# A gated mix of two attentions: left tokens laid over the key weights, output weights requested last

## The chip, the cores and the metric

The kernel runs on one NeuronCore of a Trainium2 chip (trn2). Its engines are TensorE (PE in the profile, with PEld for its weight loads), VectorE (DVE), ScalarE (ACT), GpSimd (POOL) and SyncE (SP), each with its own instruction stream; SP and ACT also request the DMA transfers here, which 16 DMA engines carry out. The metric is the device time of one execution in microseconds (us). Before the change it is 951.8 us, the median of six runs from 949.97 to 952.97.

## The reference, cut to what matters

Two attentions, A and B, are computed from the same input of 2048 tokens of 512 numbers and mixed by a gate that each token computes from itself.

```python
def _A_ref(x, mem0, Wq, Wk, Wv, Wo, seg_len):      # 32 heads of 128, 8 memory tokens, segments of 32
    mem = mem0
    for s in range(n_seg):                          # 64 segments, one after the other
        h = jnp.concatenate([mem, xs], axis=1)      # 8 memory tokens and 32 tokens
        q, k, v = h @ Wq, h @ Wk, h @ Wv            # per head
        p = softmax(where(mask, q @ k.T * scale, -1e9))
        o = (p @ v) @ Wo
        mem = o[:, :M, :]                           # the next segment's memory
        outs.append(o[:, M:, :])
def _B_ref(x, wq, wk, wv, wo, beta):               # 32 heads of 16, 4 stretches of 512 tokens
    for s in range(4):
        a_dot = softmax(qs @ ks.T * scale + mask) @ vs
        a_mem = (phi(qs) @ M) / (phi(qs) @ z + 1e-6)
        outs.append(g * a_mem + (1 - g) * a_dot)
        M = M + phi(ks).T @ vs; z = z + phi(ks).sum()
    return o @ wo
g = sigmoid((x * gate_w).sum(-1))
return g * _A_ref(...) + (1 - g) * _B_ref(...)
```

In A every segment needs the memory of the segment before, so the 64 segments form one chain. B can be computed at any time.

## The kernel before, in words

**Emission.** The kernel is planned in Python. `Prog` keeps one list of operations for each engine; an operation states which resources it reads and writes, and `emit` (line 162) turns that into semaphore waits. An engine carries its list out strictly in the order in which the plan wrote it.

**The projections (0 to about 75 us).** `plan_loads` (line 451) asks SP for the input and B's weights (wkB, wvB, wqB), and returns a list of 29 delayed requests: eight pieces of 512 KB each of Wk, Wq and Wv and four of 1 MB of Wo, requested by ACT, and at last woB, eight small requests by SP. `b_projections` (line 570) returns 64 pieces, of four stretches: keys, values and queries of B, each a product of four matmuls on PE, a cast on ACT or DVE to a staging buffer (stgk, stgq, stgp in rings of three or four; V17 for the values) and a store to a scratch in HBM by SP (kTd, qTd, pQd, vd). The last four pieces are the values of the last stretch; the last element only finishes what is outstanding. The loop at line 365 runs the pieces, and behind a piece it takes requests from the list (line 379): two behind every three pieces while more than five are left, then one behind every fifth piece. Whatever is left is requested behind the loop (line 381). Wo_sb lies over the input x_sb, so a Wo request may not come before the input has been transposed.

**Shared memory.** The buffers of the projections (`in_p`, line 282) and those of the segments (`in_a`, line 291) use the same stretch of SBUF. `v.under` (line 298) finds for each segment buffer the projection buffers under it, with a margin of 64 bytes, and the first user of a segment buffer waits for the last users of those (`over`, line 334). In bytes from the start of the stretch, a partition's share of the projection buffers is wkB 0 to 4096, wqB to 8192, wvB to 12288, V17 to 16640, phK to 20736, and small ones and the staging buffers behind. Of the segment buffers, LN_sb starts at 0, KTL at 2048, QTL at 6144, VL at 10240, xL at 14336, KN_sb at 14592, QN_sb at 16640.

**Left tokens.** The last eight tokens of each segment are called left tokens here. For four segments at a time (a group), `left_units` (line 925) copies their input to xL on POOL (line 928) and computes their K, Q and V in six products of 16 matmuls (line 911, KL0 to VL1). A product of K or Q is cast to LN_sb (line 945), by ACT or DVE as the table A_ENG says, and turned ("flipped") by a transpose on DVE (lines 923 and 949) to KTL or QTL; V is cast to VL. Group 0 is computed between the projections and segment 0; group g + 1 is spread over group g.

**A segment.** `segment` (line 1091) defines units and runs them in the order that a list names; A_ORDER (line 856) has four lists, for the four segments of a group (called the first to the fourth kind). Q, K and V are half products (Q0x, Q0y and so on), q0, k0, v0 are their casts to QN_sb, KN_sb and V_sb, TQ and TK the flips, S the scores, X the exponential, M the sums, L their reciprocals, N and n the normalising, PV and PL the products with the values, E their casts to OT_sb (line 1217), W the products with Wo (line 964), H and l the split of the result in a high and a low part, F the sum over four head groups (line 986), hm the cast of the new memory, ax that of the output rows, oL a copy of the left tokens' columns on POOL.

Other names are fillers, which put B's work and the tails between: bS (scores, line 746), bE (exponential, line 760, with a mask on POOL, line 767), bP (product with the values, line 793), bT (the rest), Fc and Ff (begin a left product or the like), Fe (its cast). A filler looks whether there is something for it to do at that point (lines 1252 to 1274) and otherwise does nothing. How many bS are due by the end of a segment is fixed (line 1250). B's keys and values come back from HBM by `load` (line 704): for the first job SP is asked for them right behind the projections (line 384).

**Banks.** PE writes to eight PSUM banks, handed out by `Banks` in the order of the plan; a product waits for the cast that emptied its bank.

Of the kernel before, what the change touches and what calls it, by code (L numbers as in the profile page):

```python
# [7 lines left out]
BF16 = mybir.dt.bfloat16  # L8
# [215 lines left out]
def build(nc, es, A_x, A_mem0, A_Wq, A_Wk, A_Wv, A_Wo, B_wq, B_wk, B_wv, B_wo, B_beta, gate_w, out, dbg=None):  # L224
# [28 lines left out]
    def sbt(name, shape, dt, stack):  # L253
        return stack.enter_context(nc.sbuf_tensor(name, shape, dt))

    def alloc(stack, *specs):
        at, spans = 0, {}
        for name, shape, dt, n in specs:
            t = [sbt(name + (str(i) if n else ""), shape, dt, stack) for i in range(max(n, 1))]
            setattr(v, name, t if n else t[0])  # L260
            size = 4 if dt == F32 else 2
            for k in shape[1:]:
                size *= k
            for i in range(max(n, 1)):
                spans[name + (str(i) if n else "")] = (at, at + size)
                at += size
        return spans
# [20 lines left out]
    v.stg = {"k": v.stgk, "q": v.stgq, "p": v.stgp}  # L288
    v.x_sb = v.Wo_sb[:, 0:NTT, :]
    esA = ExitStack()  # L290
    in_a = alloc(esA, ("LN_sb", [128, 2, 512], BF16, 0), ("KTL", [128, H // 2, SEG, 2], BF16, 2), ("QTL", [128, H // 2, SEG, 2], BF16, 2),
          ("VL", [128, 2, 512], BF16, 2), ("xL", [128, C, SEG], BF16, 0), ("KN_sb", [128, 2, 512], BF16, 0), ("QN_sb", [128, 2, 512], BF16, 0),
          ("KT_sb", [128, H // 2, SEG, 2], BF16, 0), ("QT_sb", [128, H // 2, L, 2], BF16, 0), ("V_sb", [128, 2, 512], BF16, 0),
          ("P_sb", [128, 2, 224], BF16, 0), ("R_sb", [128, 2, 160], F32, 0),
          ("OT_sb", [128, H, L], BF16, 0), ("OTL", [128, H, SEG], BF16, 2),
# [17 lines left out]
    def Rs(name):  # L313
        if name not in R:
            R[name] = Res(name)
            home = v.home(name)
            if home:
                R[name].readers = over(home)
        return R[name]
# [42 lines left out]
    weights = plan_loads(v, A_x, A_mem0, A_Wq, A_Wk, A_Wv, B_wq, B_wk, B_wv, B_wo, B_beta, gate_w)  # L362
    pieces = b_projections(v)
    bat = v.bat = BAttn(v)
    for n in range(len(pieces)):
        if n % 4 == 0 and n < 16:
            x_chunk(v, n // 4)
        if n == 9:
            sigmoid(v, v.beta_sb[:, :], v.gB_sb, v.omgB_sb, "gB", [Rs("beta")])
            for src, dst, res in ((v.gB_sb, v.gBp, "gB"), (v.omgB_sb, v.omgBp, "omgB")):  # L370
                for j in range(4):
                    q = slice(32 * j, 32 * j + 32)
                    P.op("gp", lambda g, src=src, dst=dst, q=q, j=j: g.tensor_copy(dst[q, :], src[q, :].rearrange("p (f j) -> p f j", j=4)[:, :, j]),
                         reads=[Rs(res)], writes=[Rs(res + "p")], name="%sp%d" % (res, j))
            v.late_const()
        if n == 24:
            plan_gates(v)
        pieces[n]()
        if weights and (n % 3 if len(weights) > 5 else n % 5 == 0):
            weights.pop(0)()  # L380
    while weights:
        weights.pop(0)()
# [118 lines left out]
def x_chunk(v, k):  # L501

    P, Rs, BK, C = v.P, v.Rs, v.BK, v.C
    for h in range(2):
        bk = BK.take()
        tiles = (4 * k + 2 * h, 4 * k + 2 * h + 1)

        def f(pe, bk=bk, tiles=tiles):
            ins = None
            for n, i in enumerate(tiles):  # L510
                for c in range(C):
                    o = (n * C + c) * 128
# [15 lines left out]
def sigmoid(v, src, g, o, res, reads):  # L528

    P, rg = v.P, v.Rs(res)  # L530
    P.op("act", lambda a: a.activation(g[:, :], src, ACT.Exp, scale=-1.0), reads=reads, writes=[rg], name=res + "_e")
    P.op("dve", lambda d: d.tensor_scalar(g[:, :], g[:, :], 1.0, None, op0=ALU.add), reads=[rg], writes=[rg], name=res + "_a")
    P.op("dve", lambda d: d.reciprocal(g[:, :], g[:, :]), reads=[rg], writes=[rg], name=res + "_r")
    P.op("dve", lambda d: d.tensor_scalar(o[:, :], g[:, :], -1.0, 1.0, op0=ALU.mult, op1=ALU.add), reads=[rg], writes=[v.Rs("om" + res)],
         name="om" + res)


def plan_gates(v):

    P, Rs, BK, C, NTT = v.P, v.Rs, v.BK, v.C, v.NTT  # L540
    bk = BK.take()
    P.op("pe", lambda pe, bk=bk: pe.transpose(v.pb16[bk][:, 0:C], v.gwr_sb[0:C, :], v.ident[0:C, 0:C]),
         reads=[Rs("gwr"), Rs("ident")], writes=[v.rbank[bk]], name="gwtr")
    v.evac("dve", v.gw_sb[:, :], v.pb16[bk][:, 0:C], [bk], [Rs("gw")], "gwev")
    BK.give(bk)
    bk = BK.take()

    def f_gate(pe, bk=bk):
        ins = None
        for i in range(NTT):  # L550
            for c in range(C):
                ins = pe.matmul(v.pb[bk][:, i:i + 1], v.xT[:, c, i * 128:(i + 1) * 128], v.gw_sb[:, c:c + 1],
                                start=(c == 0), stop=(c == C - 1))
        return ins
    P.op("pe", f_gate, reads=[r for k in range(4) for r in x_res(v, k)] + [Rs("gw")], writes=[v.rbank[bk]], name="gate_mm")
    sigmoid(v, v.pb[bk][:, 0:NTT], v.g_sb, v.omg_sb, "g", [v.rbank[bk]])
    BK.give(bk)
    bk = BK.take()

    def f_m0tr(pe, bk=bk):  # L560
        ins = None
        for c in range(C):
            ins = pe.transpose(v.pb16[bk][:, c * v.M:(c + 1) * v.M], v.mem0_sb[0:v.M, c * 128:(c + 1) * 128], v.ident[0:v.M, 0:v.M])
        return ins
    P.op("pe", f_m0tr, reads=[Rs("mem0"), Rs("ident")], writes=[v.rbank[bk]], name="mem0tr")
    v.evac("dve", v.hT[0][:, :, 0:v.M], v.pb16[bk][:, 0:C * v.M].rearrange("p (c t) -> p c t", t=v.M), [bk], [Rs("hTm0_0"), Rs("hTm0_1")], "memT0")
    BK.give(bk)
# [120 lines left out]
class BAttn:  # L688
# [157 lines left out]
    def finish(self, sb, f):  # L846
# [8 lines left out]

A_ORDER = [o.split() for o in (
    """
    Q0x K0x bE bE bT Q0y Fe K0y Q1x q0 bE k0 bE Q1y TQ0 bP K1x Fe bE TK0 K1y Fe S0 q1 TQ1 X0 bS V0x bS k1 M0 TK1 bE V0y S1 bE bE V1x X1 v0
    V1y M1 L0 n0 Fe Fc N0 L1 v1 PV0 PL0 N1 E0b n1 E0a Fe Fc PV1 PL1 W0a W0b E1a E1b Fe Fe W1a bE W1b bP bS H0 Fe Fe Ff Fc l0 H1 bP bE l1
    bE Fe Ff F0 hm0 ax0 bS F1 hm1 Fe oL Fe ax1 bS Ff bE Fe bE Ff""",  # L860
    """
    K0x Q0x bE bE bE Q0y K0y bE Q1x q0 Fe bE Q1y TQ0 bE Fe Fe bP k0 K1x bE q1 bE TK0 TQ1 K1y k1 bE TK1 bE S0 X0 bS Fe V0x M0 bE V0y S1 V1x
    bE L0 V1y N0 n0 Fe v0 X1 Fe M1 L1 v1 Fc PV0 n1 N1 PL0 bE Fc E0b bE E0a PV1 Fe PL1 W0a E1b bT W0b E1a W1a oL W1b Fe Fe bP H0 bS bS Fe
    Ff Fc l0 bP bP bE H1 l1 Fe bE Ff F0 bE bS hm0 F1 hm1 bS ax1 bE ax0 bE Fe""",
    """
    Q0x bT Fe Q0y q0 bE K0x bP bE TQ0 K0y k0 Q1x Q1y TK0 K1x K1y S0 q1 Fe V0x bS TQ1 Fe X0 k1 Fe TK1 M0 V0y Fe S1 bE V1x V1y L0 X1 v0 bE
    M1 L1 N0 v1 Fe Fe Fc bE PV0 N1 n0 PL0 E0b bE E0a n1 Fe bT Fc PV1 PL1 W0a W0b E1b E1a W1a W1b bE Fe Fc H0 bP l0 bS H1 Fe Ff oL bP l1 bE
    Fe F0 bS hm0 ax0 F1 Ff hm1 ax1 Fe Fe""",
    """
    Q0x Fe bS bT bE Q0y bE Fe bE q0 K0x TQ0 bP K0y bE k0 Fe Fe Fc Q1x Q1y Fc Fc q1 K1x Fc TK0 TQ1 K1y k1 TK1 S0 X0 bE bS Fe V0x M0 V0y S1  # L870
    bE V1x L0 X1 N0 Fe v0 n0 V1y Fe M1 v1 PV0 L1 N1 bE n1 bE PL0 Fe E0b PV1 Fe E0a PL1 bP W0a E1b bT W0b E1a Fe bE W1a W1b bE H0 bS bE l0
    Fe H1 Ff bP l1 Ff bT bE F0 hm0 bE ax0 bS F1 Fe bS hm1 Fe Ff ax1 Fc Fe Fe oL Ff""")]
A_ENG = dict(E0a="dve", E0b="act", E1a="act", E1b="dve", H0="act", H1="dve", K0="act", K1="dve", KL0="act", KL1="act", L0="dve",
             L1="act", OL="dve", Q0="act", Q1="act", QL0="dve", QL1="act", V0="act", V1="dve", VL0="act", VL1="dve", ax="act", hm="act",
             n="gp")


def plan_a(v, nseg):
# [13 lines left out]
    ngrp = (nseg + 3) // 4  # L892
    ORDER, ENG = DEV.get("order") or A_ORDER, DEV.get("eng") or A_ENG
    if len(ORDER) != 4:
# [503 lines left out]
```

## Time and profile before

| | us |
|---|---|
| median of six runs | 951.8 (949.97 to 952.97) |
| the profiled execution | 949.97 |
| its span in the profile | 948.2 |
| PE busy | 882.9 (93%) |
| DVE busy | 658.5 (69%) |
| ACT busy | 581.3 (61%) |
| POOL busy | 249.2 (26%) |

The profile is of one execution on the chip. Times are in us from the start of the span, in the timeline the start and the length of a merged group of equal instructions; what stands in brackets behind is how long the engine had been idle before and what ended that. L911 is line 911 of the kernel. A line with SPq or ACTq is a request of a DMA transfer, not the transfer. The granted clock is the share of full speed that PE was given. Matmul ends are modelled, so busy PE time is not PE at its peak.

### The profile page before, as it was taken

The page shows a single profiled execution, that of the slowest core. Times are in us where ns is not written, and L with a number is a line of the kernel's source. Part 1 is how long each engine was busy: PE and PEld are TensorE (multiplying, and loading weights), DVE is VectorE, ACT ScalarE, POOL GpSimd, SP SyncE. Part 2 cuts the span into 40 slices and gives each one's busy share as a digit, 9 for nine tenths or more (in the row PEclk, how much of TensorE's full clock was granted, in tenths as well). Part 3 has the DMA queues.
Part 4 walks back from the last instruction along what each step waited for, and adds up shares of the span by engine and source line. Part 5 has one row for each costly group of instructions (what it writes and reads, how often), then busy time and mean ns, then how long its engine had stood idle before and what let it go on. Part 6 is the DMA issues. An engine that isn't in the chain of part 4 may idle for free.

```text
span 948.2 us, 51802 instructions
## 1 busy us (share of the span) xinstructions
PE 882.9 (93%) x23167; PEld 467.0 (49%) x23173; DVE 658.5 (69%) x1374; ACT 581.3 (61%) x1291; POOL 249.2 (26%) x554
## 2 busy tenths in 40 slices
PE   7994989999998999999999999999999999999985
PEld 4442545545555555545555555545554555544443
DVE  3573657667676687777677687777777787777664
ACT  3352667666676666666666666666666666665443
POOL 2620223222222223232232223232322132222110
PEclk9997999999999999999999999999999999999999
DMA  9996000000001121100102011100101010000110
GB/s 297 377 383 206 5 17 17 18 18 12 24 16 38 26 50 36 29 15 18 25 15 55 26 44 24 30 22 11 42 16 49 21 44 22 26 4 9 37 37 8
DMA packets 67718, 51.38 MB, mean 54 GB/s; under 512 B 34592, under 2 KB 64424, under 8 KB 67496
## 3 DMA queue, kind: packets, MB, share of 16 engines
q1 hardware_dynamic: 59880, 31.29, 12.0%
q10 hardware_dynamic: 7616, 16.78, 4.8%
q8 instruction: 182, 2.98, 1.3%
q14 instruction: 40, 0.33, 0.1%
HBM read 33.47 MB, written 14.57 MB: 51 GB/s over the span
## 4 chain that ended last, share of the span: by engine, by line
PE 82%; DVE 8%; ACT 5%; issue 3%; DMA 2%; POOL 0%; ACTq 0%; DVEq 0%; POOLq 0%
PE ps L911 43%; PE ps L964 13%; PE ps L746 5%; PE ps L1197 3%; PE ps L630 2%; PE ps L986 2%; PE ps L605 2%; DVE WL L975 2%; ACT PT L760 2%; PE ps L1136 2%; PE ps L793 2%; PE ps L1162 2%; DMA scr_pQd<-stgp 1%; PE ps L1210 1%; PE ps L1129 1%
## 5 line engine op out<-in xcount | busy, mean ns | idle before, releaser
L760 ACT ACTIVATE PT<-ps 128x1024 bf16<-128x1024 f32 x160 | 164.0, 1025 | 7.4 <-PE ps L746 6.1
L767 POOL TENSOR_SCALAR_AFFINE_SELECT PT<-PT 128x512 bf16<-128x512 bf16 (+1 forms) x96 | 75.7, 788 | 274.9 <-ACT PT L760 261.0
L911 PE MATMUL ps<-Wv_sb,hT 128*32 128x512 bf16 x2048 | 142.9, 381 | 0.0
L911 PE MATMUL ps<-Wk_sb,hT 128*32 128x512 bf16 x2048 | 141.5, 379 | 0.0
L911 PE MATMUL ps<-Wq_sb,hT 128*32 128x512 bf16 x2048 | 138.0, 380 | 0.0
L964 PE MATMUL ps<-Wo_sb,OT_sb 128*32 128x512 bf16 x2048 | 123.2, 380 | 0.2 <-DVE OT_sb L356 0.2
L923 DVE STREAM_TRANSPOSE QT_sb<-QN_sb 128x256 f32<-128x256 f32 x128 | 56.6, 442 | 83.8 <-ACT QN_sb L354 83.8
L1187 POOL TENSOR_TENSOR P_sb<-P_sb,R_sb 128x64 bf16<-128x64 bf16 x128 | 52.8, 412 | 187.7 <-DVE R_sb L1170 77.2
L354 ACT ACTIVATE QN_sb<-ps 128x512 bf16<-128x512 f32 x128 | 76.8, 600 | 40.6 <-PE ps L911 39.7
L354 ACT ACTIVATE OT_sb<-ps 128x320 bf16<-128x320 f32 x128 | 56.0, 437 | 66.9 <-PE ps L1210 66.3
L1145 ACT ACTIVATE P_sb<-ps 128x224 bf16<-128x224 f32 x128 | 45.7, 357 | 66.5 <-PE ps L1136 65.1
L975 DVE TENSOR_TENSOR WL<-ps,WH 128x256 bf16<-128x256 f32 x128 | 54.3, 424 | 43.1 <-ACT WH L354 39.3
L356 DVE CAST OT_sb<-ps 128x320 bf16<-128x320 f32 x128 | 61.6, 482 | 26.2 <-PE ps L1210 25.7
L1170 DVE RECIPROCAL R_sb<-ps 128x160 f32<-128x160 f32 x64 | 74.1, 1157 | 7.8 <-PE ps L1162 2.6
L911 PEld LDWEIGHTS ps<-Wk_sb,hT 128*32 128x32 bf16 x2048 | 52.2, 97 | 46.0 <-ACT KN_sb L354 1.6
L911 PEld LDWEIGHTS ps<-Wq_sb,hT 128*32 128x32 bf16 x2048 | 50.5, 96 | 46.7 <-ACT hT L354 4.2
L964 PEld LDWEIGHTS ps<-Wo_sb,OT_sb 128*32 128x32 bf16 x2048 | 49.4, 96 | 44.5 <-ACT OT_sb L354 5.1
L746 PE MATMUL ps<-QTj,KTj 32*128 32x256 bf16 (+1 forms) x768 | 62.6, 254 | 3.4 <-ACT PT L760 2.7
L923 DVE STREAM_TRANSPOSE KT_sb<-KN_sb 128x256 f32<-128x256 f32 x128 | 56.6, 442 | 11.5 <-ACT KN_sb L354 7.9
L354 ACT ACTIVATE WH<-ps 128x256 bf16<-128x256 f32 x64 | 24.6, 384 | 56.6 <-PE ps L964 48.3
L354 ACT ACTIVATE LN_sb<-ps 128x512 bf16<-128x512 f32 (+1 forms) x80 | 40.6, 507 | 25.2 <-PE ps L911 14.1
L1181 DVE TENSOR_TENSOR P_sb<-P_sb,R_sb 128x160 bf16<-128x160 bf16 x128 | 45.9, 358 | 12.7 <-ACT R_sb L1177 0.9
(132 smaller groups left out, 1620.2 us busy)
## 6 DMA issues: line engine op xcount, KB each, us to landing
Wk_sb<-in_A_Wk_dram ACTq DMA_DIRECT2D x8, 512.0 KB, 6.0
Wq_sb<-in_A_Wq_dram ACTq DMA_DIRECT2D x8, 512.0 KB, 6.9
Wv_sb<-in_A_Wv_dram ACTq DMA_DIRECT2D x8, 512.0 KB, 6.8
Wo_sb<-in_A_Wo_dram ACTq DMA_DIRECT2D x4, 1024.0 KB, 11.6
scr_vd<-V SPq DMA_DIRECT2D x16, 136.0 KB, 6.2
Vj<-scr_vd SPq DMA_DIRECT2D x32, 68.0 KB, 2.4
Wo_sb<-in_A_x_dram SPq DMA_DIRECT2D x4, 512.0 KB, 7.4
scr_kTd<-stgk SPq DMA_DIRECT2D x16, 128.0 KB, 7.8
```

The lines of the kernel that those rows point to most:

```text
L354: P.op("act", lambda a: a.activation(dst, src, ACT.Copy), reads=[v.rbank[k] for k in bks], writes=dres, name=name)
L356: P.op("dve", lambda d: d.tensor_copy(dst, src), reads=[v.rbank[k] for k in bks], writes=dres, name=name)
L746: ins = pe.matmul(v.pb[bks[x]][:, 256 * e + o:256 * e + o + w], KT[e][r, 128 * kc:128 * (kc + 1)], QT[r, q0:q0 + w], start=True, stop=True ...
L760: P.op("act", lambda a: a.activation(pt[:, :, :], v.ps[:, bks[0]:bks[1] + 1, :], ACT.Exp, scale=v.SCALE_B), reads=[v.rbank[b] for b in bks ...
L767: P.op("gp", lambda g: g.affine_select(mv, mv, [[0, mv.shape[1]], [1, 128]], ALU.is_ge, 0.0, base=0, channel_multiplier=-1), reads=[rp], w ...
L911: ins = pe.matmul(pb[bk][SEG * j:SEG * (j + 1), :], lhs(c), cols(w, j) if split else w[:, 512 * j:512 * (j + 1)], start=(c == 0), stop=(c ...
L923: P.op("dve", lambda d: d.transpose(to, src), reads=reads, writes=writes, name=name)
L964: ins = pe.matmul(pb[bk][SEG * j:SEG * (j + 1), :], lhs(4 * k + j), Wo_sb[:, 4 * k + j, :], start=(first and k == ks[0]), stop=False, skip ...
L975: P.op("dve", lambda d: d.tensor_tensor(lo[:, c], pb[bk][:, c], hi[:, c], ALU.subtract), reads=[rbank[bk], Rs(res[0][hf])], writes=[Rs(res ...
L1170: P.op("dve", lambda d: d.reciprocal(R_sb[:, b, :], pb[bk][:, 224:384]), reads=[rbank[bk]], writes=[Rs("R%d" % b)], name="rcp%d_%d" % (s, b))
L1181: P.op("dve", lambda d: d.tensor_tensor(wide(P_sb, b)[:, :, 0:L], wide(P_sb, b)[:, :, 0:L], R_sb[:, b, :].rearrange("p (i q) -> p i q", q= ...
L1187: P.op(ENG["n"], lambda d: d.tensor_tensor(left(P_sb), left(P_sb), grp04(R_sb[:, b, :]), ALU.mult), reads=[Rs("R%d" % b)], writes=[Rs("P%d ...
```

## The change

Three things change. xL and LN_sb become the first two segment buffers in the shared stretch, so that xL starts at 0 and LN_sb at 256, over wkB; KTL, QTL and VL move up by 256 bytes, and KN_sb and all behind it stay. The last five requests (Wo's four and woB) are taken behind every fourth piece after piece 54, that is behind pieces 56 and 60, and what is left behind the loop; before, they were taken behind pieces 40, 45, 50, 55 and 60. And the four lists of A_ORDER are written anew, with far fewer fillers, and the cast of KL1 goes from ACT to DVE.

```diff
-    in_a = alloc(esA, ("LN_sb", [128, 2, 512], BF16, 0), ("KTL", [128, H // 2, SEG, 2], BF16, 2), ("QTL", [128, H // 2, SEG, 2], BF16, 2),
-          ("VL", [128, 2, 512], BF16, 2), ("xL", [128, C, SEG], BF16, 0), ("KN_sb", [128, 2, 512], BF16, 0), ("QN_sb", [128, 2, 512], BF16, 0),
+    in_a = alloc(esA, ("xL", [128, C, SEG], BF16, 0), ("LN_sb", [128, 2, 512], BF16, 0), ("KTL", [128, H // 2, SEG, 2], BF16, 2), ("QTL", [128, H // 2, SEG, 2], BF16, 2),
+          ("VL", [128, 2, 512], BF16, 2), ("KN_sb", [128, 2, 512], BF16, 0), ("QN_sb", [128, 2, 512], BF16, 0),
...
-        if weights and (n % 3 if len(weights) > 5 else n % 5 == 0):
+        if weights and (n % 3 if len(weights) > 5 else n > 54 and n % 4 == 0):
...
-    Q0x K0x bE bE bT Q0y Fe K0y Q1x q0 bE k0 bE Q1y TQ0 bP K1x Fe bE TK0 K1y Fe S0 q1 TQ1 X0 bS V0x bS k1 M0 TK1 bE V0y S1 bE bE V1x X1 v0
-    V1y M1 L0 n0 Fe Fc N0 L1 v1 PV0 PL0 N1 E0b n1 E0a Fe Fc PV1 PL1 W0a W0b E1a E1b Fe Fe W1a bE W1b bP bS H0 Fe Fe Ff Fc l0 H1 bP bE l1
-    bE Fe Ff F0 hm0 ax0 bS F1 hm1 Fe oL Fe ax1 bS Ff bE Fe bE Ff""",
+    K0x Q0x bE bT Q0y K0y Q1x q0 Q1y k0 TQ0 TK0 bP K1x K1y S0 q1 X0 TQ1 k1 bS V0x M0 bE V0y v0 TK1 L0 N0 S1 V1x X1 V1y M1 v1 L1 n0 Fc PV0
+    PL0 E0b n1 N1 E0a Fe Fc PV1 PL1 W0a E1a W0b E1b W1a Fe W1b bP bS Ff Fc H0 bP l0 H1 bE l1 Fe Ff F0 hm0 ax0 bS F1 hm1 Fe ax1 Ff Fe oL""",
...
-    Q0x Fe bS bT bE Q0y bE Fe bE q0 K0x TQ0 bP K0y bE k0 Fe Fe Fc Q1x Q1y Fc Fc q1 K1x Fc TK0 TQ1 K1y k1 TK1 S0 X0 bE bS Fe V0x M0 V0y S1
-    bE V1x L0 X1 N0 Fe v0 n0 V1y Fe M1 v1 PV0 L1 N1 bE n1 bE PL0 Fe E0b PV1 Fe E0a PL1 bP W0a E1b bT W0b E1a Fe bE W1a W1b bE H0 bS bE l0
-    Fe H1 Ff bP l1 Ff bT bE F0 hm0 bE ax0 bS F1 Fe bS hm1 Fe Ff ax1 Fc Fe Fe oL Ff""")]
-A_ENG = dict(E0a="dve", E0b="act", E1a="act", E1b="dve", H0="act", H1="dve", K0="act", K1="dve", KL0="act", KL1="act", L0="dve",
+    Q0x bS bT Q0y bE q0 bP K0x TQ0 K0y k0 Q1x TK0 Q1y q1 K1x TQ1 K1y k1 S0 bS V0x TK1 X0 M0 bE V0y S1 L0 N0 V1x V1y n0 X1 v0 M1 PV0 PL0 v1
+    L1 N1 E0b PV1 n1 E0a PL1 E1b bP W0a bT W0b W1b E1a W1a H0 l0 bS H1 bE Ff l1 bP bT oL F0 bS F1 hm0 ax0 Fe hm1 Ff ax1""")]
+A_ENG = dict(E0a="dve", E0b="act", E1a="act", E1b="dve", H0="act", H1="dve", K0="act", K1="dve", KL0="act", KL1="dve", L0="dve",
```

The lists of the second and third kind, left out here, change in the same manner. Taken engine by engine, with fillers that find nothing to do left aside, the steps that stand elsewhere are these. First kind: K0x ahead of Q0x, v0's cast ahead of X1, KL1's cast on DVE behind E1b, the exponential and mask of the last bS of the segment behind POOL's two copies that open the next segment. Third and fourth kind: one bP ahead of K0x instead of behind it, and in the fourth W1b ahead of W1a. Where a bank's earlier holder changes, the set of casts that a step waits for is nearly always the same. In the first and second kind, oL and a mask of B change places in POOL's list.

## The prediction

> **What bounds the kernel now.** The sum of the page comes first: PE is busy 93% of a span of 948.2 us, and 82% of the chain that ended last is PE. Idle PE time is what a change can win, so the next view is the table of busy time by stage.
>
> ```profile
> 60.00:70.00 10.00, 10.00 (x48) 4.51 (x46) 6.76 (x14) 4.91 (x8) 0.00 (x0) 1.00 1.09 382
> 70.00:80.00 10.00, 3.35 (x15) 1.37 (x14) 5.53 (x11) 3.43 (x6) 0.00 (x0) 0.92 1.09 383
> 80.00:90.00 10.00, 4.43 (x56) 2.10 (x60) 0.84 (x3) 1.20 (x2) 0.29 (x1) 0.57 0.43 133
> 90.00:100.00 10.00, 10.00 (x283) 5.66 (x272) 7.13 (x14) 5.63 (x11) 2.28 (x6) 1.00 0.11 16
> ...
> 120.00:920.00 800.00, 765.58 (x21392) 406.12 (x21384) 578.70 (x1212) 516.01 (x1159) 211.76 (x433) 1.00 0.11 26
> ```
>
> The columns are PE, PEld, DVE, ACT, POOL, the granted clock, DMA share and GB/s. The 800 us of segments hold 34 us of idle PE, 0.56 us a segment. The seam between the projections and the segments holds 12.2 us in one piece, with the clock down to 0.57 behind it, and the DMA engines are full until 80. The timeline of the seam says why.
>
> ```profile
> 77.96 0.43 SPq L583 DMA_DIRECT2D scr_vd<-V  x1
> 78.44 4.20 SPq L496 DMA_DIRECT2D woB_sb<-in_B_wo_dram  x8
> 82.68 0.90 SPq L583 DMA_DIRECT2D scr_vd<-V  x2
> 83.63 1.85 SPq L716 DMA_DIRECT2D KTj<-scr_kTd  x4
> 85.18 0.29 POOL L928 COPY xL<-xT 128x128 bf16<-128x128 bf16 x1 [29.48 <-DMA scr_vd<-V]
> 85.52 0.53 SPq L716 DMA_DIRECT2D QTj<-scr_qTd  x1
> ...
> 85.57 3.36 PE L911 MATMUL ps<-Wk_sb,xL 128*32 128x512 bf16 x32 [12.16 <-issue]
> ...
> 88.75 1.91 PE L911 MATMUL ps<-Wq_sb,xL 128*32 128x512 bf16 x32
> ```
>
> PE's last projection matmul ends at 73.41 and the next one starts at 85.57. It reads xL, whose copy on POOL waits for the last two stores of V17 (scr_vd). Those stand on SP behind eight requests of woB (4.20 us), and they land at 85.15. The waits from 66 to 92 us show the second delay, ahead of the stores:
>
> ```profile
> POOL xL L928 <- DMA scr_vd<-V: 29.5, 1, 29.5
> ...
> ACT stgq L354 <- DMA scr_qTd<-stgq: 5.1, 4, 1.7
> DVE stgp L594 <- DMA scr_pQd<-stgp: 4.6, 5, 1.3
> ```
>
> ACT and DVE wait for staging buffers whose 128 KB stores take 5.0 to 7.0 us to land, because Wo shares the DMA engines (from 62 to 68.8 us its queue has 56.3%, SP's 52.6%). So the last V casts end at 75.47 on ACT and 78.17 on DVE, long after PE's 73.41.
>
> **Part 1, the layout.** By the sizes in the code wkB covers bytes 0 to 4096 of the shared stretch and V17 12288 to 16640. xL moves from 14336 to 0, LN_sb to 256. Their only earlier owner is then wkB, whose last reader is the last key projection, over on PE at about 68.9. POOL is idle from 60 to 80, so the 0.29 us copy is done by 69.3. VL (10496 to 14592) and KN_sb still lie over V17: the wait does not vanish, it moves from the first left matmul to the casts of the left values.
>
> PE can thus start at 73.5. The six left products cost 5.2 us: from 88.75 to the next segment's first matmul at 92.20 are four of them, 0.86 each. The first two took 3.18 us (85.57 to 88.75) where two warm ones take 1.72; 1.46 of that is the cold clock (0.50 from 85 to 88), which goes with the idle time. Segment 0 starts at 78.7, not at 92.20: **13.5 us earlier**, before new waits.
>
> **Part 2, the requests.** Reading the loop, Wo's four requests come after pieces 40, 45, 50, 55 before (54.5, 59.4, 63.7, 68.9 in the trace), after 56 and 60 and the end behind it; woB's eight go behind the last V store. Issuing costs ACT nothing new. Without Wo, SP's stores are the only load from about 58, 0.39 MB in each 1.73 us of PE, 227 of the 383 GB/s seen. DVE needs 1.66 us for such a pair (0.69 + 0.28 + 0.69), so it keeps step. The last V casts then end at about 73.2 (DVE) and 74.0 (ACT), and the last V store is issued by 74.5, not at 83.2. PE itself gains nothing there, it is full from 60 to its end.
>
> What is late next? Three arrivals.
>
> *V17's stores.* Landing took 1.9 us in quiet (82.7) and 4.1 to 6.1 beside Wo (74 to 79): landed between 76.4 and 80.6. The left V casts would run at 78; they block ACT's cast of q0, due at 80.2, only if the stores land after 79.6. At most 1 us, and the next wait swallows it.
>
> *The first job's keys.* SP issues woB from 74.5 to 78.7 (4.20), then four KTj and one QTj (1.85 + 0.05 + 0.53) to 81.1. Quiet, these landed 1.7 to 2.8 us after issue; beside Wo a store took 4.1 to 6.1. The first bS stands on PE right behind S0, at 96.08 before, 82.6 now. The keys land between 83.4 and 87.2; I take 84.5, between the quiet row and 4.1, as these are small and their queue has no backlog. Stall **1.9 us**, ends 0.8 and 4.6. Its V half (Vj) is issued by 85.3 and first read about 91.5: covered.
>
> *Wo.* From 68.9 on there are 4.19 MB of Wo, 0.52 of woB, 1.07 of last stores and 0.39 of job loads: 6.2 MB, at 383 GB/s 16.1 us, landed at 85.0. The first reader, W0a, was at 101.30 and would be at 89.7. Covered by 4.7 us; without that cover its lateness counts one for one.
>
> The Trainium skill, "DMA: Bandwidth & Descriptors", section "Queues, rings and completion order", speaks against this part: each DMA engine alternates between queues packet by packet, so weights asked for late halve the rate of the last stores and first loads; the shares above show that. The same page, section "Anatomy of one DMA — SWDGE (gpsimd) path", fits a transfer of the software path (these are issued by SP) at 2.0 us plus its bytes over 436 GB/s; an estimate by it puts the keys at 83.2 and the stall at 0.6, a gain of 12.9.
>
> **Part 3, the order.** Most words struck from the lists are fillers that found nothing to do. Comparing what remains engine by engine, few steps differ, in one kind of segment each.
>
> ```profile
> 417.62 0.20 PEld L1197 LDWEIGHTS ps<-P_sb,V_sb 32*128 32x128 bf16 x16 [0.47 <-ACT R_sb L1177]
> ...
> 419.77 0.59 ACT L354 ACTIVATE LN_sb<-ps 128x512 bf16<-128x512 f32 x1
> ...
> 420.39 0.45 DVE L923 STREAM_TRANSPOSE KTL<-LN_sb 128x256 f32<-128x256 f32 x1 [0.40 <-ACT LN_sb L354]
> ```
>
> The first kind's KL1 cast goes from ACT (0.59) to DVE (0.68, as its other LN_sb casts), 15 times and once ahead of segment 0. DVE is free there from 420.0, so cast and flip end at 421.1; its next work is at 421.66 and waits for ACT. Hidden; if it were not, 10.2 us. The cast v0 now goes ahead of X1, which delays the sums by about 0.12 us, 16 times, 1.9; but PV0 at 417.62 waits for v1 (DVE, to 417.51), so I take nothing. W1b before W1a in the fourth kind: both casts end by 406.57, the product that reads them starts at about 406.9; at best it removes half of the 4.7 us for which PEld waited for OT_sb. bP half a pass earlier in the third and fourth kinds reads a PT masked a few us before; the later oL is read a group later. POOL has time for both (26%). Sum **0**, ends 2.3 won and 1.9 lost.
>
> **Sum.** 13.5 - 1.9 + 0 = 11.6 us. Everything behind the seam is bound by PE and tied segment to segment, and the number of B steps due by each segment is unchanged, so the shift is carried to the end. The profiled execution took 949.97 (span 948.2), giving 938.4; the median of the six runs is 951.8, 0.2% higher, and the prediction is 951.8 - 11.6 = **940.2**.
>
> **Rivals.** *The V17 wait only moves* (9%). For it: VL and KN_sb still lie over V17. If the stores landed as late as before, at 85.15, the left V cast would take ACT to 85.8, and S0, which came 1.92 after the start of q0's cast, would be at 87.7 for 95.65: 7.9 us won, 943.9. Against it: woB's 4.20 us leave its place ahead of them, and the buffer waits go.
>
> *Wo comes late, still faster* (4%). At the 206 GB/s of the page's fourth slice the 6.2 MB take 30.1 us, landed at 99.0, 9.3 late: 2.3 won, 949.5. Against it: the queues together made 380 or more whenever both had work.
>
> *Slower* (3%): the same wait in front of W0a, one for one. It decides once Wo lands after 103.2, that is below 181 GB/s over the whole backlog. At 170 it lands at 105.4, 15.7 late: 955.9. For it: Wo's queue has only half of the engines while SP's has work. Against it: SP's has only 2 MB.
>
> *No difference* (2%): Wo at 101, between those two.
>
> **Numbers.** My forecast has 82%: 940.2, from 936.8 (13.5 - 0.8 + 2.3 won) to 944.8 (13.5 - 4.6 - 1.9). That range takes in the first rival and leaves out the others and the tails, so it is the range I give. Faster by more than 0.2% (1.9 us, about what a measurement can tell): 82 + 9 + 4 = 95%; within: 2%; slower: 3%.
>
> **What would show it.** Right: the POOL copy of xL near 69; no PE gap of more than 1 us from 73 to 79, clock 1.0 through it; left products of 0.86 each; a PE wait of 1 to 4 us at the first bS put down to the KTj or QTj loads; W0a not waiting; PE's idle time in the segments about 0.56 us each. Wrong: stores of V17 landing after 81; the first Wo product waiting for the DMA; DVE or the sums later in every first or fourth segment.

## The result, and the profile after

The changed kernel takes 947.4 us (median of 21 runs, 943.6 to 951.3) where the kernel before takes 951.7 (45 runs, 948.2 to 954.1): a ratio of 0.9956, 95% interval 0.9947 to 0.9965. It is faster by 4.2 us of 952, with 3.3 to 5.0 in the interval, and not by 11.6; 947.4 lies above the range. The profiled execution took 946.5 (span 944.8). Of all executions told of here one was slow (1681.8 us, of the run "all of it together"), and it is left out of the times.

First the table of busy time by stage, with the columns of before (PE, PEld, DVE, ACT, POOL, granted clock, DMA share, GB/s). The line numbers of the changed kernel differ a little: its L907, L960 and L1125 are L911, L964 and L1129 of before.

```profile
70.00:80.00 10.00, 9.36 (x115) 4.14 (x113) 3.69 (x7) 3.02 (x6) 0.50 (x2) 1.00 0.96 304
80.00:90.00 10.00, 4.36 (x102) 2.03 (x104) 5.75 (x12) 3.25 (x7) 0.67 (x2) 0.87 1.13 277
90.00:100.00 10.00, 10.00 (x240) 4.61 (x240) 5.63 (x11) 4.88 (x10) 2.47 (x6) 0.79 0.34 80
120.00:920.00 800.00, 765.47 (x21412) 405.36 (x21398) 587.74 (x1227) 507.65 (x1147) 211.16 (x432) 1.00 0.11 26
```

The segments are what they were (765.47 of PE against 765.58). From 70 to 80 the hole is gone. A smaller one stands between 80 and 90, with the DMA engines full through all of it, and the clock falls in it. The timeline of the seam:

```profile
69.92 0.29 POOL L924 COPY xL<-xT 128x128 bf16<-128x128 bf16 x1 [14.38 <-PE ps L605]
...
74.05 1.91 PE L907 MATMUL ps<-Wk_sb,xL 128*32 128x512 bf16 x32
...
74.16 5.38 ACTq L486 DMA_DIRECT2D Wo_sb<-in_A_Wo_dram  x2
...
76.00 4.84 SPq L496 DMA_DIRECT2D woB_sb<-in_B_wo_dram  x8
...
79.64 0.60 ACT L354 ACTIVATE LN_sb<-ps 128x512 bf16<-128x512 f32 x1 [4.88 <-PE ps L907]
...
80.29 0.61 PE L907 MATMUL ps<-Wk_sb,hT 128*32 128x512 bf16 x8 [0.88 <-ACT LN_sb L354]
...
80.89 2.03 SPq L716 DMA_DIRECT2D KTj<-scr_kTd  x4
...
82.88 0.60 ACT L354 ACTIVATE VL<-ps 128x512 bf16<-128x512 f32 x1 [0.48 <-PE ps L907]
82.96 0.54 SPq L716 DMA_DIRECT2D QTj<-scr_qTd  x1
...
85.03 0.28 PE L1125 MATMUL ps<-mneg,ident 128*32 128x224 bf16 x4 [0.48 <-ACT QN_sb L354]
...
89.96 0.61 PE L746 MATMUL ps<-QTj,KTj 32*128 32x256 bf16 x4 [4.43 <-DMA QTj<-scr_qTd]
```

xL is copied at 69.9, and PE goes from the projections into the left products at 74.05 with no gap. Then three things come late. ACT stands 5.38 us in its last two requests of Wo, and its first left cast comes at 79.64. The left V casts come at 82.88. The first bS waits 4.43 us for the keys, although PE had S0 at 85.03. The waits of this stretch name that one alone as a DMA:

```profile
ACT LN_sb L354 <- PE ps L907: 4.9, 1, 4.9
...
PE ps L746 <- DMA QTj<-scr_qTd: 4.4, 1, 4.4
```

How long a transfer takes from request to landing is in the last column of the DMA issues from 66 to 96 us. Before:

```profile
Wo_sb<-in_A_Wo_dram ACTq DMA_DIRECT2D x1, 1024.0 KB, 12.1
...
scr_vd<-V SPq DMA_DIRECT2D x4, 136.0 KB, 3.1
...
woB_sb<-in_B_wo_dram SPq DMA_DIRECT2D x8, 64.0 KB, 2.6
...
KTj<-scr_kTd SPq DMA_DIRECT2D x8, 16.0 KB, 1.9
QTj<-scr_qTd SPq DMA_DIRECT2D x2, 64.0 KB, 2.7
```

After:

```profile
Wo_sb<-in_A_Wo_dram ACTq DMA_DIRECT2D x4, 1024.0 KB, 13.8
...
scr_vd<-V SPq DMA_DIRECT2D x4, 136.0 KB, 6.1
woB_sb<-in_B_wo_dram SPq DMA_DIRECT2D x8, 64.0 KB, 6.7
Vj<-scr_vd SPq DMA_DIRECT2D x2, 68.0 KB, 8.1
KTj<-scr_kTd SPq DMA_DIRECT2D x8, 16.0 KB, 6.8
QTj<-scr_qTd SPq DMA_DIRECT2D x2, 64.0 KB, 6.9
```

The keys' 16 KB now take 6.8 us instead of 1.9. The last QTj of the job's first half is asked for at 82.96 and lands 6.9 later, at 89.9: that is the bS at 89.96. V17's last store is asked for at about 75.6; the store issued there took 7.3 to land, 82.9: that is the left V cast at 82.88. The row of that cast names PE, but PE had ended those products at 79.4; where the engine named has long been done, another releaser has to be looked for.

**The ledger.** Let the seam run from PE's last projection product to W0a, the first product with Wo. Before it is 27.89 us (73.41 to 101.30); the prediction's marks make it 16.2 (73.5 to 89.7, with the 1.9 of stall), and after it is 22.94 (74.05 to 96.99). S0, the first bS and W0a of before, and W0a after:

```profile
95.65 0.28 PE L1129 MATMUL ps<-mneg,ident 128*32 128x224 bf16 x4
...
96.08 0.39 PE L746 MATMUL ps<-QTj,KTj 32*128 32x256 bf16 x4
...
101.30 1.91 PE L964 MATMUL ps<-Wo_sb,OT_sb 128*32 128x512 bf16 x32
```

```profile
96.99 1.91 PE L960 MATMUL ps<-Wo_sb,OT_sb 128*32 128x512 bf16 x32
```

| step on PE | planned | after | late by |
|---|---|---|---|
| projections end | 73.5 | 74.05 | 0.55 |
| from there to S0 (5.2 + 3.45) | 8.65 | 10.98 | 2.3 |
| S0 to the first bS (0.43 + 1.9) | 2.3 | 4.93 | 2.6 |
| first bS to W0a | 5.2 | 7.03 | 1.8 |

Together 7.3 us late, and 11.6 - 7.3 = 4.3: W0a is 4.31 us earlier than before. By the ratio of all executions the time is 4.2 lower, and between the two profiled ones, which are single executions, the span is 3.4 lower (948.2 to 944.8). So the seam alone explains what went missing up to W0a, and behind it the two traces differ by 0.9.

### The profile page after: what moved, and what is told of

It reads as the page before. It is cut to its first block, busy times and chain, and to the rows that moved or that the text cites. A ratio compares the mean times of both kernels' runs of the same rounds, so it can differ in the third digit from the quotient of the medians.

```text
span 944.8 us, 51801 instructions
## 1 busy us (share of the span) xinstructions
PE 886.4 (94%) x23167; PEld 466.3 (49%) x23173; DVE 668.1 (71%) x1390; ACT 572.7 (61%) x1275; POOL 249.4 (26%) x554
## 3 DMA queue, kind: packets, MB, share of 16 engines
q8 instruction: 182, 2.98, 1.3%
## 4 chain that ended last, share of the span: by engine, by line
PE 84%; DVE 7%; ACT 5%; issue 2%; DMA 1%; SPq 1%; POOL 0%; ACTq 0%; DVEq 0%; POOLq 0%
PE ps L907 42%; PE ps L960 14%; PE ps L746 5%; PE ps L605 3%; PE ps L1193 3%; PE ps L630 3%; PE ps L982 2%; ACT PT L760 2%; DVE WL L971 2%; PE ps L1132 2%; PE ps L1158 2%; PE ps L793 2%; PE ps L1206 1%; PE ps L1125 1%; PE ps L1128 1%
## 5 line engine op out<-in xcount | busy, mean ns | idle before, releaser
L907 PE MATMUL ps<-Wv_sb,hT 128*32 128x512 bf16 x2048 | 144.6, 384 | 0.0
L907 PE MATMUL ps<-Wk_sb,hT 128*32 128x512 bf16 x2048 | 138.5, 380 | 0.9 <-ACT LN_sb L354 0.9
L907 PE MATMUL ps<-Wq_sb,hT 128*32 128x512 bf16 x2048 | 135.6, 380 | 0.4 <-DVE LN_sb L356 0.4
L960 PE MATMUL ps<-Wo_sb,OT_sb 128*32 128x512 bf16 x2048 | 123.7, 380 | 0.4 <-DVE OT_sb L356 0.4
L907 PEld LDWEIGHTS ps<-Wq_sb,hT 128*32 128x32 bf16 x2048 | 51.3, 96 | 50.8 <-ACT hT L354 4.2
L907 PEld LDWEIGHTS ps<-Wk_sb,hT 128*32 128x32 bf16 x2048 | 51.1, 97 | 44.0 <-ACT KN_sb L354 1.6
L960 PEld LDWEIGHTS ps<-Wo_sb,OT_sb 128*32 128x32 bf16 x2048 | 49.5, 96 | 45.2 <-ACT OT_sb L354 5.2
L1193 PEld LDWEIGHTS ps<-P_sb,V_sb 32*128 32x128 bf16 x2048 | 24.1, 91 | 60.4 <-ACT OT_sb L354 33.8
```

The source lines that it names most:

```text
L907: ins = pe.matmul(pb[bk][SEG * j:SEG * (j + 1), :], lhs(c), cols(w, j) if split else w[:, 512 * j:512 * (j + 1)], start=(c == 0), stop=(c ...
L960: ins = pe.matmul(pb[bk][SEG * j:SEG * (j + 1), :], lhs(4 * k + j), Wo_sb[:, 4 * k + j, :], start=(first and k == ks[0]), stop=False, skip ...
L1193: ins = pe.matmul(pb[bks[j]][:, L * i:L * (i + 1)], V_sb[SEG * j:SEG * (j + 1), b, i * E:(i + 1) * E], P_sb[SEG * j:SEG * (j + 1), b, LW * ...
```

## The experiments

**The theories.** K: the first job's keys are late, because they queue behind woB on SP and their packets share the engines with Wo; the late bS and the cold clock behind it are the main loss. R: ACT is stuck in the two requests of Wo, and S0 is late for it. O: the new order of the segments costs something. In the first four runs each part of the change is put alone on the kernel before, and the keys are moved in the changed kernel.

**The layout alone**, on the kernel before (requests and order as before).

```diff
-    in_a = alloc(esA, ("LN_sb", [128, 2, 512], BF16, 0), ("KTL", [128, H // 2, SEG, 2], BF16, 2), ("QTL", [128, H // 2, SEG, 2], BF16, 2),
-          ("VL", [128, 2, 512], BF16, 2), ("xL", [128, C, SEG], BF16, 0), ("KN_sb", [128, 2, 512], BF16, 0), ("QN_sb", [128, 2, 512], BF16, 0),
+    in_a = alloc(esA, ("xL", [128, C, SEG], BF16, 0), ("LN_sb", [128, 2, 512], BF16, 0), ("KTL", [128, H // 2, SEG, 2], BF16, 2), ("QTL", [128, H // 2, SEG, 2], BF16, 2),
+          ("VL", [128, 2, 512], BF16, 2), ("KN_sb", [128, 2, 512], BF16, 0), ("QN_sb", [128, 2, 512], BF16, 0),
```

> The kernel before with the layout alone: xL and LN_sb first, the requests and the order as before. Theory K (the whole change lost its gain at the first bS, to keys that land late behind woB and beside Wo: 4.4 us of waiting and about 1.8 us of cold clock behind it): here Wo is asked for early, so V17's stores land at 85.15 as before, the left V casts wait for them, S0 stands at about 87.7 and the keys land at 88.3 as before. 6 to 8 us won, ratio 0.992 to 0.994, more than the whole change. Theory R (the loss comes from ACT, which was stuck 5.4 us in the last two Wo requests): the same here, since no request is late. Theory O (the new order costs what the seam wins): the full 13.5 us less the wait for V17, so also 7 to 8. This run prices the layout and the V17 rival; it tells K and R from nothing, but it must lie above 1 to 3 us if any of them is right.

Measured: 946.05 us, ratio 0.9936 (0.9920 to 0.9952), 6.1 us won. One part of the change wins more than the whole by the medians, though the two intervals still touch. In its profile the keys are there when bS comes (87.62, no wait), and the wait on V17 has moved, as the first rival had it:

```profile
77.73 4.68 SPq L496 DMA_DIRECT2D woB_sb<-in_B_wo_dram  x8
...
82.45 0.90 SPq L583 DMA_DIRECT2D scr_vd<-V  x2
...
84.93 0.60 ACT L354 ACTIVATE VL<-ps 128x512 bf16<-128x512 f32 x1 [6.12 <-DMA scr_vd<-V]
...
87.08 0.38 PE L1129 MATMUL ps<-mneg,ident 128*32 128x224 bf16 x4 [4.21 <-ACT QN_sb L354]
```

The last two stores of V17 stand behind woB as before the change, ACT's left V cast waits 6.12 us for them, and S0 comes at 87.08 (that rival had said 87.7, and 7.9 us won). Behind the wait of 4.21 us the clock is 0.50 from 88 to 92, so that W0a comes 7.70 us after bS and not 5.22.

**The requests alone**, on the kernel before.

```diff
-        if weights and (n % 3 if len(weights) > 5 else n % 5 == 0):
+        if weights and (n % 3 if len(weights) > 5 else n > 54 and n % 4 == 0):
```

> The kernel before with the moved requests alone: layout and order as before. xL still waits for V17's stores. By all theories they are issued by 76 and land near 82, so the first left product starts about 3 us earlier, at 82 to 83. K: the keys land near 90, S0 would stand at about 92, so they are covered: 3 us won, ratio 0.997. R: ACT is stuck in the requests until 79.5, before the left products start, so it costs nothing here either: 3 us. If both layout and requests win what is stated here, their sum is larger than what the two together won, 4.3 us, and the missing part is the collision.

Measured: 948.82, ratio 0.9960 (0.9947 to 0.9973), 3.8 us won. The left products still wait for V17, which lands earlier now: the gap ahead of them is 7.97 us instead of 12.16. It was expected to win 3. Alone the two parts win 6.1 and 3.8, together 4.2: they get in each other's way.

**The order alone**, on the kernel before: the four new lists and the cast of KL1.

```diff
-    Q0x K0x bE bE bT Q0y Fe K0y Q1x q0 bE k0 bE Q1y TQ0 bP K1x Fe bE TK0 K1y Fe S0 q1 TQ1 X0 bS V0x bS k1 M0 TK1 bE V0y S1 bE bE V1x X1 v0
+    K0x Q0x bE bT Q0y K0y Q1x q0 Q1y k0 TQ0 TK0 bP K1x K1y S0 q1 X0 TQ1 k1 bS V0x M0 bE V0y v0 TK1 L0 N0 S1 V1x X1 V1y M1 v1 L1 n0 Fc PV0
...
-A_ENG = dict(E0a="dve", E0b="act", E1a="act", E1b="dve", H0="act", H1="dve", K0="act", K1="dve", KL0="act", KL1="act", L0="dve",
+A_ENG = dict(E0a="dve", E0b="act", E1a="act", E1b="dve", H0="act", H1="dve", K0="act", K1="dve", KL0="act", KL1="dve", L0="dve",
```

> The kernel before with the new order of the units and the KL1 cast on DVE alone. K and R: nothing, ratio 0.998 to 1.002, the seam unchanged with its gap of 12.2 us. O: slower by 5 us or more, ratio 1.005 or above, with more idle PE time than 34 us between 120 and 920.

Measured: 953.21, ratio 1.0007 (0.9997 to 1.0018). The gap is there as before (12.37), PE is busy for 765.67 us from 120 to 920. O, which asked for 5 us or more, falls: the order costs at most 1.7 us by the interval, and nothing that can be seen.

**The keys ahead of woB**, in the changed kernel.

```diff
-    while weights:
+    while len(weights) > 1:
         weights.pop(0)()
     for part in "kv":
         for G in range(2):
             bat.load(0, G, part)
+    while weights:
+        weights.pop(0)()
```

> The changed kernel with one thing moved: woB's eight requests go behind the requests for the first job's keys and values, not ahead of them; Wo's requests on ACT stay. K: the keys are asked for at 76 instead of 80.9, land by 84, the first bS finds them or waits under 1 us, and the clock stays up: 4.4 + 1.8 us more than the change won, near 941, ratio to the kernel before 0.988 to 0.991. R: ACT is stuck as long as before, and the total stays where the change left it, ratio 0.995 to 0.996.

Measured: 943.91, ratio 0.9912 (0.9896 to 0.9928), 8.4 us won, about twice the change. Moving five microseconds of SP's requests behind twelve small ones wins the lost bS back:

```profile
83.37 0.28 PE L1127 MATMUL ps<-mneg,ident 128*32 128x224 bf16 x4 [1.32 <-ACT QN_sb L354]
...
83.80 0.39 PE L748 MATMUL ps<-QTj,KTj 32*128 32x256 bf16 x4
...
87.38 0.21 PE L1195 MATMUL ps<-P_sb,V_sb 32*128 32x40 bf16 x5
...
90.38 0.25 PE L1195 MATMUL ps<-P_sb,V_sb 32*128 32x40 bf16 x11 [2.79 <-issue]
```

bS follows S0 by 0.43 us, with no wait. But a new pause stands in the first PV: after five of its 16 matmuls PE stops for 2.79 us, and the profile finds nothing that it waited for. With it the time is some 3 us above the 941 that K had asked for.

**Wo's last two requests on SP, at their old place in the order**, in the changed kernel. ACT is free of them, and the keys come still later, since these requests stand ahead of woB and the keys on SP: what is good by R is bad by K.

```diff
-  name="dma_Wo%d" % q, eng="act")
+  name="dma_Wo%d" % q, eng="act" if q < 2 else "sp")
```

> The changed kernel with Wo's last two requests made by SP instead of ACT at the same place in the plan, ahead of woB and of the first job's keys. ACT is free for the left casts, SP carries the long requests. R (ACT stuck in the requests costs the gain): the left casts run from 75, segment 0 starts at 79.2 and its S0 near 82.5, 2 us or more better than the change, near 945. K (the keys cost it): the keys are asked for later by as much as SP is held up, up to 5 us, so the first bS waits longer than the 4.4 us seen, and the total is worse than the change by 2 to 5 us, near 950, although S0 comes earlier.

Measured: 950.24, ratio 0.9974 (0.9961 to 0.9987): 2.5 us won, less than the change. ACT is not stuck any more, and the time is worse:

```profile
76.87 8.23 SPq L496 DMA_DIRECT2D woB_sb<-in_B_wo_dram  x8
...
81.12 0.60 ACT L354 ACTIVATE VL<-ps 128x512 bf16<-128x512 f32 x1 [4.04 <-DMA scr_vd<-V]
...
83.27 0.28 PE L1125 MATMUL ps<-mneg,ident 128*32 128x224 bf16 x4 [1.72 <-ACT QN_sb L354]
...
91.80 0.61 PE L746 MATMUL ps<-QTj,KTj 32*128 32x256 bf16 x4 [8.04 <-DMA QTj<-scr_qTd]
```

Now SP is the one that is stuck (8.23 us in woB's eight requests), the keys are asked for from 85.1 on, and the first bS waits 8.04 us. K holds in both directions. S0 stands 10.54 us behind the projections' end (72.73) instead of 10.98: freeing ACT alone brings 0.4 us. The VL row says why: V17's stores are as late as ACT was, and hold the left V casts all the same. So R is one of two reasons for the late S0, and taking it away uncovers the other.

**The keys first, and woB not until segment 4**: does the traffic of woB cause the pause in PV? To the edit of the keys ahead of woB comes:

```diff
-    while weights:
-        weights.pop(0)()
+    v.late_wob = weights
...
             if s < nseg:
+                if s == 4:
+                    v.late_wob.pop(0)()
                 next_tail(1)
```

> The changed kernel with woB's eight requests made only at segment 4, its first reader being some eighteen segments in; keys first, Wo's requests on ACT as in the change. Against the run with the keys first this takes woB's 0.52 MB, written to 16 partitions at a time, away from Wo's transfer. In that run PE stood still for 2.8 us in the middle of a group of 16 matmuls at 87.4 with nothing to wait for, beside a DMA share of 1.13 and a rate fallen to 280 GB/s. If that pause comes from the traffic (an instruction load among it), it goes or shrinks and the time falls by 2 to 3 us to about 941; if it has nothing to do with the DMA, the time stays at 944. K and R both predict no change at the first bS.

Measured: 944.47, ratio 0.9908 (0.9888 to 0.9928), 8.8 us won, as with woB directly behind the keys. The pause is there, 2.52 us, behind the same fifth matmul: woB is not its cause. Here the clock falls behind the pause too, to 0.50 from 90 to 92.

**Wo as early as before the change, woB at segment 4**, with the new layout and order; woB is kept back as in the run before this one. If the late request of Wo is not needed for the gain, nothing is lost here.

```diff
-        if weights and (n % 3 if len(weights) > 5 else n > 54 and n % 4 == 0):
+        if len(weights) > 1 and (n % 3 if len(weights) > 5 else n % 5 == 0):
```

> The layout and the order of the change, Wo requested as early as before (behind pieces 40, 45, 50, 55), and only woB moved, to segment 4. The stores of V17 then stand behind no request; the staging buffers wait as before, so the last V cast ends at 78, its store lands near 81 to 82 and the keys, asked for from 79, near 83 to 84. S0 near 84.5 and no wait at bS: about 11 us earlier than before, W0a near 90, no request holds ACT. K and R: 940 to 942, better than the change by 5 to 7 us. If instead asking for Wo late is worth more than its collisions, this run is no better than the keys first, 944.

Measured: 943.76, ratio 0.9900 (0.9881 to 0.9920), 9.5 us won, and 1.8 us above the far end of what was expected. V17's stores hold the left V casts for 2.67 us, S0 stands at 86.11; behind it there is no wait at bS, no pause in PV (one group of 16), no cold clock, and W0a stands at 91.92. The late request of Wo is not what wins: with woB out of the way, asking for Wo early is at least as good (9.5 against 8.8 in the run before, with intervals that overlap).

**All of it together**: the first job's loads directly behind the last V store, Wo's last two requests on SP behind them, woB kept back to segment 4 by the lines shown above.

```diff
-    while weights:
-        weights.pop(0)()
     for part in "kv":
         for G in range(2):
             bat.load(0, G, part)
+    while len(weights) > 1:
+        weights.pop(0)()
+    v.late_wob = weights
...
-  name="dma_Wo%d" % q, eng="act")
+  name="dma_Wo%d" % q, eng="act" if q < 2 else "sp")
```

> The change with all three collisions taken away: the first job's keys right behind the V stores, Wo's last two requests behind them and on SP, woB at segment 4. K and R: S0 near 82.5, the keys landed by 83, so about 13 us won at the first bS; Wo's last 2 MB are asked for from 80.6 and land near 87 to 88, just about when W0a wants them (88.3). 939 to 941. If Wo lands later than that its lateness shows as a wait of the first Wo product for the DMA.

Measured: 943.19, the median of the five executions counted, ratio 0.9913 (0.9890 to 0.9935), 8.3 us won, and 2.2 us above the far end of what was expected. Its trace tells nothing of the seam, so the kernel was run a second time.

> The kernel of e8 a second time, since no usable trace of it was had: the first job's loads straight behind the last V store, Wo's last two requests on SP behind them, woB at segment 4. If the keys (K) and ACT's time in the requests (R) are all that was lost, S0 stands at 83 or before, the first bS does not wait, PE does not pause, W0a begins at about 90 and the time is 940 to 942. If instead PE pauses inside the first PV products as in e4 and e6 (2.5 to 2.8 us with nothing to wait for, while Wo is in flight), or W0a waits for the Wo that SP asks for last, W0a stands at 92 to 94 and the time is 943 to 945, as e8 gave.

Measured: 944.09, ratio 0.9906 (0.9891 to 0.9921), 9.0 us won: the second of the two cases.

```profile
75.84 0.60 ACT L354 ACTIVATE LN_sb<-ps 128x512 bf16<-128x512 f32 x1 [0.39 <-PE ps L907]
...
83.24 0.60 ACT L354 ACTIVATE VL<-ps 128x512 bf16<-128x512 f32 x1 [4.15 <-PE ps L907]
...
85.39 0.28 PE L1125 MATMUL ps<-mneg,ident 128*32 128x224 bf16 x4 [1.83 <-ACT QN_sb L354]
...
85.82 0.39 PE L746 MATMUL ps<-QTj,KTj 32*128 32x256 bf16 x4
...
92.39 0.28 PE L1193 MATMUL ps<-P_sb,V_sb 32*128 32x40 bf16 x11 [2.79 <-issue]
```

ACT casts LN at 75.84 at once, so nothing is left of R, and yet S0 is 10.65 us behind the projections' end (74.74). The left V casts start on ACT and DVE in the same moment, 83.2, which is when V17's last store lands (asked for at 75.9, 7.2 us). Then PE pauses in PV as before.

**The keys first, with the old order**: does the pause belong to the new order? On top of the keys ahead of woB, the lists and the cast go back:

```diff
-    K0x Q0x bE bT Q0y K0y Q1x q0 Q1y k0 TQ0 TK0 bP K1x K1y S0 q1 X0 TQ1 k1 bS V0x M0 bE V0y v0 TK1 L0 N0 S1 V1x X1 V1y M1 v1 L1 n0 Fc PV0
+    Q0x K0x bE bE bT Q0y Fe K0y Q1x q0 bE k0 bE Q1y TQ0 bP K1x Fe bE TK0 K1y Fe S0 q1 TQ1 X0 bS V0x bS k1 M0 TK1 bE V0y S1 bE bE V1x X1 v0
...
```

> The kernel of e4 (the change, with woB behind the first job's loads) with the order lists and the engine of the cast of KL1 as before. Theory K with an order that is worth nothing: the time of e4, about 8 us under the kernel before (942 to 946), W0a within 0.5 us of 91.9. Rival: the new order pays or costs once the seam is mended, so that this is over 2 us away from e4, in the segments, with W0a in its place. It also tells whether PE's pause inside the first PV products (2.79 us in e4) belongs to the new order: with the old one it is there at the same product, or it is gone.

Measured: 945.13, ratio 0.9924 (0.9909 to 0.9938), 7.2 us won; against the new order's 8.4 the intervals overlap. The pause is there (2.85 us, at the same matmul). W0a stood at 93.58 and not within 0.5 of 91.9, but the projections had ended at 74.30 instead of 72.35 in this execution: the seam is 19.28 us long here and 19.57 there.

**All of them by one measure.** The end of the projections wanders from 70.8 to 75.8 between the profiled executions, also of kernels that hardly differ up to there. The length of the seam is the better measure, and what is won in it agrees with the ratios to 1.4 us.

| kernel | S0 behind the projections' end | bS behind S0 | W0a behind bS | seam | won in it | won by the ratio |
|---|---|---|---|---|---|---|
| before | 22.24 | 0.43 | 5.22 | 27.89 | | |
| layout alone | 14.10 | 0.54 | 7.70 | 22.34 | 5.5 | 6.1 |
| requests alone | 19.04 | 0.43 | 5.23 | 24.70 | 3.2 | 3.8 |
| order alone | 22.31 | 0.43 | 5.34 | 28.08 | -0.2 | -0.7 |
| the change | 10.98 | 4.93 | 7.03 | 22.94 | 4.9 | 4.2 |
| Wo by SP | 10.54 | 8.53 | 7.22 | 26.29 | 1.6 | 2.5 |
| keys first | 11.02 | 0.43 | 8.12 | 19.57 | 8.3 | 8.4 |
| woB at segment 4 | 10.67 | 0.44 | 7.89 | 19.00 | 8.9 | 8.8 |
| Wo early | 11.77 | 0.44 | 5.37 | 17.58 | 10.3 | 9.5 |
| all | 10.65 | 0.43 | 9.06 | 20.14 | 7.8 | 9.0 |
| keys first, old order | 10.68 | 0.43 | 8.17 | 19.28 | 8.6 | 7.2 |

Each wait that is taken away uncovers the next. The four kernels with the new layout that ask for Wo late and have their keys in time lose 2.7 to 3.8 us in the column of W0a: to the pause, and in one to the cold clock behind it. In two of them cold clock also falls behind W0a, where this measure does not see it: the 32 products with Wo take 3.42 us with woB at segment 4 and 3.61 with all together, instead of 1.91. From W0a to the end the single executions take from 846.9 us (before) to 850.3 (Wo early), and most of that spread is not explained.

**What the pause is** was not settled by an experiment of its own; the traces give one reading. A queue that the profile calls "instruction" moves some 16 KB in a packet (182 packets, 2.98 MB in the profile before); I take it to load instructions. In the four kernels that pause, such a packet moves only 3.6 to 3.9 us after the first bS (87.5, 85.75, 89.75 and 89.0, read in steps of 0.25), as the pause begins, and PE goes on 2.5 to 3.0 us later. With Wo early, so that the engines are nearly free, it moves 0.45 us after bS (87.0), PE reaches the same product 3.1 us later, and does not stop. In the changed kernel it moves at 90.0, beside the bS that had waited 4.43 us. That fits a load of instructions that is asked for before bS, is held up by the full DMA engines, and hid behind the wait for the keys in the changed kernel. One thing sits less well: with woB at segment 4 the DMA share fell to 0.15 half a microsecond after the pause had begun (86 to 86.5), and PE stood on to 88.22. No run changed the instruction load alone, so this stays an argument.

## Why the prediction was wrong

**Right.** Why PE stood idle, and that the layout ends it: xL copied near 69 (69.9), no gap from 73 to 79, clock 1.0, left products at 0.86 (74.05, then 75.78 and 77.51 for each two). The first segment product comes 11.9 us earlier. The order is worth nothing that can be seen (order alone, 1.0007; segments 765.47 against 765.58). W0a does not wait for Wo, though by luck, as told below. The shift is carried to the end: 4.3 us at W0a, 4.2 in the time by the ratio.

**Wrong, and decisive: the first job's keys.** "I take 84.5, between the quiet row and 4.1, as these are small and their queue has no backlog"; they landed at 89.9, beyond the far end of 87.2 too. 1.9 us of it is the asking (82.96 against 81.1): SP was through woB at 80.89 and not at 78.7, since its last V stores went out 1.5 us later (76.0) and woB took 4.84 instead of 4.20. The rest is the landing: 6.9 us, where the slowest row that I had used for them was 6.1, although the same prediction had read 5.0 to 7.0 for stores beside Wo. Nor was their queue without a backlog: woB's eight requests stood ahead on it. Yet without those, in the run of all together, the 16 KB still took 5.3 us. Being small did not help: 16 KB took as long as 64 KB. The stall was 4.43 us where 1.9 stood in the sum. Keys first, and Wo by SP, show that this is the term: taking it away doubles the gain, and making it worse (8.04 us) takes 1.7 us of the gain away.

**Wrong: the backlog's rate.** "6.2 MB, at 383 GB/s 16.1 us, landed at 85.0". From 69 to 90 the engines moved 6.1 MB, 289 GB/s, at a mean share of 1.03: 380 from 75 to 80, with Wo and SP's stores in flight, and 277 from 80 on, with Wo, woB and the small loads. Wo alone moved no more, 289 from 73 to 74 at a share of 1.05, so 383 held only for the mix that it was read from. Wo's last part landed at 94.2, 19.6 us after its request. W0a, which waits for all of Wo, stood at 96.99 and was saved by the other delays; at the forecast 89.7 it would have waited, so the cover of 4.7 us was not there. With the requests in this order the forecast 940.2 could not have been reached.

**Wrong: V17's stores**, "landed between 76.4 and 80.6 ... At most 1 us". The last landed at 82.9, after 81, which the prediction named as a sign against itself. It is the same backlog again.

**Wrong: "Issuing costs ACT nothing new."** The rows of before show a request of Wo at about 0.4 us, with the earlier ones spaced out by 5 us. Of four within 5 us the last held ACT for 4.96 us. This and V17's stores overlap, and as far as the rows show either alone puts S0 where it stood to within half a microsecond: without the hold on ACT it came 0.44 us sooner (Wo by SP, 10.54 against 10.98), and with it ACT waited only 0.48 us more at the left V cast. Together they are the 2.3 us.

**Missing: the clock.** The prediction counted the 1.46 us of cold clock that go with the old gap, and put a stall into the new seam without asking the same of it. In the 4.43 us of waiting the clock fell to 0.50:

```profile
86.00:88.00 2.00, 0.00 (x0) 0.00 (x0) 0.45 (x1) 0.03 (x1) 0.00 (x0) 0.84 1.12 247
88.00:90.00 2.00, 0.04 (x2) 0.07 (x4) 0.00 (x0) 0.00 (x0) 0.00 (x0) 0.50 1.13 297
90.00:92.00 2.00, 2.00 (x28) 0.79 (x32) 0.22 (x1) 1.02 (x1) 0.30 (x1) 0.50 1.12 288
92.00:94.00 2.00, 2.00 (x56) 1.03 (x52) 1.41 (x2) 0.84 (x2) 0.65 (x2) 0.50 0.51 101
```

From 90 to 94 PE is at work at half speed; W0a is 1.8 us further from bS than before. The Trainium skill, "TensorE: Matmul & The Clock Gate", section "Part 1: The HAM clock gate", says that the clock halves after an idle window of about 3.4 us, that the window runs freely, and that as much work brings it back. The 4.43 us here are longer than that, and the clock stayed at 0.50 until 94, after some 4 us of work. The shorter waits do not fit an idle window of that length: the clock here was falling before 88 already (0.84 from 86 to 88), within 2.5 us of PE's last matmul, which ended at 85.5; and a pause of 2.79 us left it at 1.00 with the keys first (88 to 92) but took it to 0.50 in the run of all together (92 to 94). There the measurement decides: 2.8 us can be enough.

**The rule that spoke against the change.** The page of the Trainium skill that the prediction weighed ("DMA: Bandwidth & Descriptors", section "Queues, rings and completion order") says that each DMA engine goes round the queues that have work, packet by packet. The landings fit that a full queue beside their own delays small loads, and by more than half: 6.8 us for 16 KB instead of 1.9. The estimate by the same page's fit of 2.0 us plus the bytes (section "Anatomy of one DMA — SWDGE (gpsimd) path"), which is for another path than SP's, had put the keys at 83.2; they landed at 89.9, and the measurement decides.

## What to carry to other kernels

When transfers are moved later to free an early stage, list what is requested in the stage that they land in, in the order of the queues, and price each small load at the longest landing that the trace shows beside a full queue, or above it; then put the loads that are read first ahead of the big ones that are read last, which here doubled the gain (8.4 us against 4.2). A stall that goes into a forecast can bring its cold clock with it: 4.4 us did here, and pauses of 2.5 to 2.9 did in two kernels and did not in two. And try the parts of a change alone: here one part won 6.1 us and the whole 4.2, so the later requests, as they stood, took about a third of it away (by the medians; the intervals touch).

## What the runs showed that was not expected

A request of a DMA is not always cheap on an engine that has asked for much: 0.4 us for most requests of 1 MB, but 4.6 to 5.4 us for the last two in the five kernels that ask for all four from ACT late, and 8.23 us for eight of 64 KB on SP behind two of 1 MB (4.0 to 4.8 otherwise). At a full share the 16 DMA engines moved 382 GB/s in one mix, 277 in another and 289 with Wo alone. And PE can stop in the middle of a group of matmuls for 2.5 to 2.9 us with nothing in the program to wait for, in four kernels at the same instruction, each time with the DMA engines full as it began.
